# Copying the columns of the triangular inverse's outer products to PSUM in three parts

## The chip, the cores and the metric

The kernel runs on one core of one Trainium2 chip, as one program of five engines that work at the same time: TensorE (PE) for matrix products, VectorE (DVE), ScalarE (ACT) and GpSimd (POOL) for elementwise work, and SyncE (SP), which issues most DMAs. The metric is the device time of one execution in microseconds; the median of several executions is compared.

## What is computed

Three parts follow each other: an attention with a recurrent state, a layer of eight experts with one expert for each token, and a last layer of two products with a leaky ReLU. The change lies in the first part:

```python
def _attn_ref(r, k, v, w, a, b):
    for t in range(S):
        y[:, :, t] = einsum('bhd,bhde->bhe', rt, state)
        Sa = einsum('bhde,bhe->bhd', state, at)
        state = state * wt[:, :, None, :] - einsum('bhd,bhe->bhde', Sa, bt)
        state = state + einsum('bhd,bhe->bhde', vt, kt)
```

Here B = 4, H = 8, S = 768 and D = 40, all in float32. The expert layer has 3072 tokens of 320 values and 1024 hidden values for an expert, the last layer 2048 hidden values.

## The kernel before, in words

The recurrence is computed in chunks of `C` = 64 time steps. Inside a chunk the steps depend on each other through a lower triangular matrix, so each chunk needs the inverse of a unit triangular matrix of 64 x 64. Two batches and 256 time steps (four chunks) make one group; there are six groups, each with eight slots (four chunks, two halves of the heads), 48 slots in all. While the slots of one group run, the next group is prepared: `prepare` (decays by two scans on DVE, L455 and L457, and the scaled k, b and a, L460 and L464, on POOL), `products` (the matrices of a chunk, copied out of PSUM by ACT at L484 and L485 and masked by DVE at L491), and `inverse`. Each slot itself has stages that TensorE, ACT and DVE work on in turn: `stage_a` (L640, L642, L645), `stage_v` (L611, L613, L614), `stage_r` (L624, L628, L630), `stage_p` (L600, L602), `stage_c` (L656, L660, L661), `stage_d` (L676, L677), `stage_e` (L667, L671).

`inverse` treats a 64 x 64 triangle as two of 32 x 32. All triangles of 32 x 32 of a group are inverted at once: a transpose on DVE (L522) brings them into a tile `ul` of 128 partitions by 32 x 32, so that each partition holds one matrix. Then 31 steps follow, each an outer product (L529) of what is below the diagonal in column `j` of the matrix with the first `j + 1` values of row `j` of the unfinished inverse `ut`, into `tmp`, and a subtraction of `tmp` from the rows below (L531). Step `j` has `(31 - j) * (j + 1)` elements a partition, 31 to 256. Both are DVE instructions, and each depends on the one ahead of it. After the steps two checks on ACT (L424) and two transposes on DVE (L537, L538) follow, and then the halves are merged with products on TensorE (`zp` and `yp`, L557 and L565).

`ul` and `ut` lie in SBUF. `tmp` is a tile of 256 float32 values a partition in PSUM, in the one bank of tag `mg`, which the merges' `zp` and `yp` use too. Only the first group (`o.start`) differs: its `ut` lies in PSUM and its `tmp` in SBUF.

The program's order within each engine is not written by hand after the first group: a scheduler that goes through the program with estimates of its own sorts the instructions of each engine, and adds waits on semaphores where an instruction needs another engine's result or buffer. Each engine then works through its list strictly in order. `start_inverse` asks for the steps of group i + 1 at the first slot of group i. The dependencies are kept for each tile, a PSUM tile being one bank.

Of the kernel before, what the change touches and what calls it, by code (L numbers as in the profile page):

```python
# [8 lines left out]
F32 = mybir.dt.float32  # L9
# [10 lines left out]
P = 128  # L20
# [263 lines left out]
class Attention:  # L284
# [230 lines left out]
    def inverse(self, o):  # L515

        nc = self.nc
        l1, l2 = o.l1, o.l2
        o.tt = [self.ringed("tt", self.tt) for _ in range(2)]
        ut = self.ut0 if o.start else self.unit()  # L520
        ul = self.pa.tile([P, 32, 32], F32, name="ul", tag="t4", bufs=3)
        nc.vector.transpose(ul, l2.rearrange("p c u j -> p j (c u)"))  # L522
        yield
        for j in range(31):
            n, m = 31 - j, j + 1
            if j == 0 or o.start:
                tmp = self.pa.tile([P, 256], F32, name="tmp", bufs=1) if o.start else self.work("tmp", [P, 256], "mg")
            tv = tmp[:, :n * m].rearrange("p (a b) -> p a b", b=m)
            nc.vector.tensor_tensor(tv, ul[:, j, j + 1:].unsqueeze(2).to_broadcast([P, n, m]),  # L529
                                    ut[:, j, :m].unsqueeze(1).to_broadcast([P, n, m]), op=ALU.mult)  # L530
            nc.vector.tensor_tensor(ut[:, j + 1:, :m], ut[:, j + 1:, :m], tv, op=ALU.subtract)  # L531
            if j % 2:
                yield
        self.check(ut, ul, 0.01)
        self.check(l1.rearrange("p c u j -> p (c u) j"), ul, 0.01)
        t11, ttc = self.t4("t11"), self.t4("ttc")
        nc.vector.transpose(ttc.rearrange("p c u t -> p t (c u)"), ut)  # L537
        nc.vector.transpose(t11.rearrange("p c u s -> p s (c u)"), ut.rearrange("p t s -> p s t"))  # L538
        for half in range(2):
            for q in (1, 3, 0, 2):  # L540
                r = slice(32 * q, 32 * q + 32)
                eng = nc.vector if o.start and half == 0 else nc.gpsimd
                eng.tensor_scalar(o.tt[half][r, :, :, 32 * q:32 * q + 32], ttc[r, 2 * half:2 * half + 2], 1.0, 0.0, op0=ALU.mult, op1=ALU.add)
        yield

        lows = [slice(q * 64, q * 64 + 32) for q in range(2)]
        highs = [slice(q * 64 + 32, q * 64 + 64) for q in range(2)]
        both = [(c2, u, q) for c2 in range(2) for u in range(8) for q in range(2)]
        for half in range(2):
            if half:  # L550
                yield
            tt = o.tt[half]
            zp = self.work("zp", [P, 2, 8, 32], "w1" if o.start else "mg")
            if o.start:
                self.fill(zp, 8)
            for c2, u, q in both:
                nc.tensor.matmul(zp[lows[q], c2, u], lhsT=l1[highs[q], 2 * half + c2, u, :], rhs=tt[highs[q], c2, u, highs[q]], start=True, stop=True)  # L557
            z = self.pa.tile([P, 2, 8, 32], F32, name="z1", tag="z1", bufs=1)
            for lo in lows:
                nc.scalar.copy(z[lo], zp[lo])  # L560
            yp = self.work("yp", [P, 2, 8, 32], "w1" if o.start else "mg")
            if o.start:
                self.fill(yp, 8)
            for c2, u, q in both:
                nc.tensor.matmul(yp[lows[q], c2, u], lhsT=t11[lows[q], 2 * half + c2, u, :], rhs=z[lows[q], c2, u, :], start=True, stop=True)  # L565
            for lo, hi in zip(lows, highs):
                nc.scalar.activation(tt[lo, :, :, hi], yp[lo], AF.Copy, scale=-1.0)
            yield
# [755 lines left out]
```

## Time and profile before

| what | value |
| --- | --- |
| median of 3 runs | 1153.29 us (1152.75 to 1153.30) |
| the profiled execution, its own time | 1149.13 us |
| its span, first to last instruction | 1147.3 us |
| mean granted TensorE clock | 0.937 of full speed |
| PE busy | 1016.7 us, 89% of the span |
| DVE busy | 715.6 us, 62% |
| ACT busy | 568.4 us, 50% |
| POOL busy | 548.5 us, 48% |

The profile shows one execution. The attention takes about the first 515 us, the other two parts the rest. "Busy" is the time in which an engine has an instruction running, waits inside an instruction included. Shares over the whole span say little of one stretch, so the views below are cut to stretches. In the view of the chain, the work that ended last is followed back step by step to what released it, and each step is put down to an engine and a line; "issue" is time in which the engine waited for nothing that the profile shows.

### The profile page before, as it was taken

Reading aid. Unit: us, or ns where it says so; the run is one execution under the profiler, and the core shown is the slowest. Engines: PE = TensorE matmul, PEld = TensorE weight load, DVE = VectorE, ACT = ScalarE, POOL = GpSimd, SP = SyncE. Lnnn points to the kernel's source line nnn. Section 1 sums busy time; section 2 is a strip of 40 time slices with the busy share of each in tenths; the row PEclk is TensorE's granted clock in tenths of the full one; section 3 lists DMA queues with packets and bytes.
Section 4 is the critical chain, followed back from the end, with each engine's and each line's share of the span. In section 5 each row is a group of like instructions: output and inputs, shape, how many; then the busy total and the mean of one; then the engine's idle time right before and its main releaser. Section 6 shows DMA issues by size and latency. Waiting matters only on the chain.

```text
span 1147.3 us, 24800 instructions
## 1 busy us (share of the span) xinstructions
PE 1016.7 (89%) x9597; PEld 895.2 (78%) x9597; DVE 715.6 (62%) x1469; ACT 568.4 (50%) x1426; POOL 548.5 (48%) x496
## 2 busy tenths in 40 slices
PE   2649788989899889798898889999999999999997
PEld 2538677867687777687787779999998999999996
DVE  8865887878959869444599984324444545354542
ACT  3637577867787878783554444442222212121211
POOL 6717367555675724233655535452434343434332
PEclk7659899988999999799999989999999999999999
DMA  4613223322322213525688775431000000000000
GB/s 118 203 52 96 63 56 91 89 69 69 94 85 69 56 41 76 137 60 172 179 279 256 242 236 168 131 116 38 24 24 23 23 24 24 23 23 19 29 1 26
DMA packets 98080, 103.35 MB, mean 90 GB/s; under 512 B 58404, under 2 KB 78884, under 8 KB 97956
## 3 DMA queue, kind: packets, MB, share of 16 engines
q1 hardware_dynamic: 95652, 93.83, 28.5%
q0 software_dynamic: 2304, 7.87, 2.1%
q8 instruction: 78, 1.28, 0.5%
q14 instruction: 46, 0.38, 0.1%
HBM read 79.39 MB, written 22.28 MB: 89 GB/s over the span
## 4 chain that ended last, share of the span: by engine, by line
PE 57%; DVE 22%; ACT 6%; issue 5%; DMA 5%; POOL 3%; SPq 0%; DVEq 0%; ACTq 0%; POOLq 0%
PE ph L238 20%; PE po L238 19%; DVE tmp L529 3%; PE lp L483 3%; PE pp L600 2%; DVE ut L531 2%; PE sa L640 2%; PE yc L656 2%; DMA raw<-in_moe_w_dram 2%; DVE s L455 2%; DVE dec L215 2%; DVE dec L218 1%; PE rp L628 1%; DVE q L457 1%; DVE dec L214 1%
## 5 line engine op out<-in xcount | busy, mean ns | idle before, releaser
L229 POOL TENSOR_TENSOR gl<-g,gh 128x512 fp32r<-128x512 f32 x96 | 123.9, 1293 | 211.2 <-ACT gh L228 127.1
L228 ACT ACTIVATE gh<-g 128x512 fp32r<-128x512 f32 x96 | 60.7, 632 | 249.4 <-DVE g L1214 174.5
L1213 DVE TENSOR_SCALAR g<-ph,al 128x512 f32<-128x512 f32 x96 | 72.1, 751 | 156.9 <-POOL gl L229 79.1
L238 PE MATMUL ph<-x2thi,win 128*128 128x512 f32 x480 | 157.0, 392 | 0.0
L238 PE MATMUL po<-wout,gh 128*128 128x320 f32 x768 | 139.1, 309 | 0.0
L238 PEld LDWEIGHTS po<-wout,gh 128*128 128x128 f32 x768 | 122.0, 188 | 5.4
L238 PE MATMUL ph<-x2tlo,win 128*128 128x512 f32 x288 | 113.5, 394 | 0.0
L238 PE MATMUL po<-we,hh 128*128 128x320 f32 (+1 forms) x480 | 91.5, 319 | 19.1 <-DVE hh L1089 13.4
L238 PE MATMUL ph<-xthi,we 128*128 128x448 f32 (+2 forms) x360 | 98.2, 344 | 2.8 <-DVE hl L1089 2.1
L238 PEld LDWEIGHTS ph<-x2thi,win 128*128 128x128 f32 x480 | 88.5, 188 | 13.2
L238 PEld LDWEIGHTS po<-we,hh 128*128 128x128 f32 (+1 forms) x480 | 74.5, 183 | 24.7 <-DVE hh L1089 14.8
L529 DVE TENSOR_TENSOR tmp<-ul,ut 128x31 f32<-128x31 f32 (+15 forms) x186 | 81.4, 437 | 3.7
L238 PE MATMUL po<-wout,gl 128*128 128x320 f32 x384 | 82.9, 311 | 0.0
L614 POOL TENSOR_SCALAR_AFFINE_SELECT va<-vg 64x512 f32<-64x512 f32 x48 | 35.2, 734 | 85.2 <-ACT vg L613 55.8
L238 PE MATMUL ph<-xtlo,we 128*128 128x448 f32 (+2 forms) x216 | 74.1, 344 | 0.3 <-DVE xtlo L271 0.3
L238 PEld LDWEIGHTS ph<-xthi,we 128*128 128x128 f32 x360 | 67.0, 196 | 7.0 <-issue 2.5
L464 POOL TENSOR_TENSOR abd<-ra,q 40x512 f32<-40x512 f32 x44 | 62.4, 1418 | 18.9 <-DVE q L457 5.3
L483 PE MATMUL lp<-kb,abd 128*128 128x128 f32 x352 | 56.4, 307 | 16.7 <-DMA wz<-in_wP_dram 10.7
L1214 DVE SCALAR_TENSOR_TENSOR g<-ph,g 128x512 f32<-128x512 f32 x96 | 66.3, 691 | 3.1
L656 PE MATMUL yc<-va,kbr 128*40 128x104 f32 (+3 forms) x768 | 57.2, 265 | 11.8 <-issue 8.5
L600 PE MATMUL pp<-tt,la 128*104 128x128 f32 x384 | 61.4, 309 | 6.1 <-DVE lg L902 4.1
L677 POOL TENSOR_TENSOR yt<-rs,q 104x256 f32<-104x256 f32 x46 | 34.4, 748 | 67.6 <-DVE rs L676 54.5
(212 smaller groups left out, 2358.0 us busy)
## 6 DMA issues: line engine op xcount, KB each, us to landing
raw<-in_moe_w_dram SPq DMA_DIRECT2D x16, 512.0 KB
rv<-in_rvP_dram SPq DMA_DIRECT2D x48, 160.0 KB
raw<-in_moe_w_dram SPq DMA_DIRECT2D x16, 480.0 KB
kb<-in_kbP_dram SPq DMA_DIRECT2D x44, 160.0 KB
r<-in_moe_w_in_dram SPq DMA_DIRECT2D x10, 512.0 KB
r<-in_moe_w_out_dram SPq DMA_DIRECT2D x10, 512.0 KB
xs_d<-tt SPq DMA_DIRECT2D x8, 560.0 KB
raw<-in_moe_w_dram SPq DMA_DIRECT2D x16, 256.0 KB
```

What stands on the lines that cost most here:

```text
L228: nc.scalar.activation(hi, src, AF.Copy)
L229: return lo_eng.tensor_tensor(lo, src, f32(hi), op=ALU.subtract)
L238: return nc.tensor.matmul(out, lhsT=lhsT, rhs=rhs, start=start, stop=stop)
L464: nc.gpsimd.tensor_tensor(abd[r, :, q * C:(q + 1) * C], ra[r], qc[r, :, :C], op=ALU.mult)
L483: nc.tensor.matmul(lp[:, i], lhsT=abd[:, i, c2, :], rhs=kb[:, i, c2, :], start=True, stop=True)
L529: nc.vector.tensor_tensor(tv, ul[:, j, j + 1:].unsqueeze(2).to_broadcast([P, n, m]), ut[:, j, :m].unsqueeze(1).to_broadcast([P, n, m]), op ...
L600: nc.tensor.matmul(pp[:, i], lhsT=o.la[x.half][:, x.c2, u, :], rhs=o.tt[x.half][:, x.c2, u, :], start=True, stop=True)
L614: nc.gpsimd.affine_select(x.va[:C].rearrange("p a b c -> p (a b) c")[:, :, D:], x.vg[:C].rearrange("p a b c -> p (a b) c")[:, :, D:], patt ...
L656: nc.tensor.matmul(x.yc[r, i, a:], lhsT=kb[:, c], rhs=x.va[:, i, q, a:], start=True, stop=True)
L677: eng.tensor_tensor(yt[:PP, :, x.c2 * C:x.c2 * C + C], x.rs, x.o.q[x.half][:, x.p4, x.c2, :C], op=ALU.mult)
L1213: nc.vector.tensor_scalar(g, ph, 0.0, al[:, f:f + 1], op0=ALU.min, op1=ALU.mult)
L1214: nc.vector.scalar_tensor_tensor(g, ph, 0.0, g, op0=ALU.max, op1=ALU.add)
```

## The change

The steps of the five groups after the first read their column no longer from `ul` in SBUF, but from a copy in PSUM. The tile of tag `mg` grows from 256 to 512 values a partition, which is a whole bank: `tmp` is its first half, and the second half holds a part of `ul`. ACT copies that part three times in an inverse: ahead of step 0 the columns 0 to 7 (8 x 32 values), ahead of step 8 the columns 8 to 15 from row 8 on (8 x 24), ahead of step 16 the columns 16 to 31 from row 16 on (16 x 16). Each part is written over the one before. That is 15 new ACT instructions in the program. The first group's inverse is as before.

```diff
--- before.py
+++ after.py
@@ -523,10 +523,20 @@
         yield
         for j in range(31):
             n, m = 31 - j, j + 1
-            if j == 0 or o.start:
-                tmp = self.pa.tile([P, 256], F32, name="tmp", bufs=1) if o.start else self.work("tmp", [P, 256], "mg")
+            if o.start:
+                tmp = self.pa.tile([P, 256], F32, name="tmp", bufs=1)
+                col = ul[:, j, j + 1:]
+            else:
+                if j == 0:
+                    bank = self.work("tmp", [P, 512], "mg")
+                    tmp = bank[:, :256]
+                if j in (0, 8, 16):
+                    j0, j1 = j, (8, 16, 32)[j // 8]
+                    part = bank[:, 256:256 + (j1 - j0) * (32 - j0)].rearrange("p (a b) -> p a b", b=32 - j0)
+                    nc.scalar.copy(part, ul[:, j0:j1, j0:])
+                col = part[:, j - j0, j + 1 - j0:]
             tv = tmp[:, :n * m].rearrange("p (a b) -> p a b", b=m)
-            nc.vector.tensor_tensor(tv, ul[:, j, j + 1:].unsqueeze(2).to_broadcast([P, n, m]),
+            nc.vector.tensor_tensor(tv, col.unsqueeze(2).to_broadcast([P, n, m]),
                                     ut[:, j, :m].unsqueeze(1).to_broadcast([P, n, m]), op=ALU.mult)
             nc.vector.tensor_tensor(ut[:, j + 1:, :m], ut[:, j + 1:, :m], tv, op=ALU.subtract)
             if j % 2:
```

The new lines move what follows: the product, L529, is L539 in the changed file, the subtraction L531 is L541, and the copy is L536. The scheduler sorts the engines anew.

On DVE, at the start of the first pipelined inverse (the second group), this stood (`ul` is the matrix, `ut` the inverse, `tmp` the product; in brackets the engines whose progress an instruction waits for):

```order
L522 STREAM_TRANSPOSE ul<-l_670 128x1024 [waits Pool_49]
L529 TENSOR_TENSOR tmp<-ul,ut 128x31 [waits DVE_49]
L531 TENSOR_TENSOR ut<-ut,tmp 128x31 [waits DVE_49]
L529 TENSOR_TENSOR tmp<-ul,ut 128x60 [waits DVE_49]
L531 TENSOR_TENSOR ut<-ut,tmp 128x30x2 [waits DVE_49]
```

and now:

```order
L522 STREAM_TRANSPOSE ul<-l_670 128x1024 [waits Pool_49]
L539 TENSOR_TENSOR tmp<-tmp,ut 128x31 [waits Activation_49]
L541 TENSOR_TENSOR ut<-ut,tmp 128x31 [waits DVE_49]
L539 TENSOR_TENSOR tmp<-tmp,ut 128x60 [waits DVE_49]
L541 TENSOR_TENSOR ut<-ut,tmp 128x30x2 [waits DVE_49]
```

The first product now waits for ACT, right behind the transpose that ACT's copy needs, with nothing in between.

At steps 7 and 8 of the same inverse DVE had:

```order
L531 TENSOR_TENSOR ut<-ut,tmp 128x25x7 [waits DVE_49]
L457 SCALAR_TENSOR_TENSOR q<-wz_106,d1q_119 104x520 [waits DVE_49]
L529 TENSOR_TENSOR tmp<-ul,ut 128x192 [waits DVE_49]
L531 TENSOR_TENSOR ut<-ut,tmp 128x24x8 [waits DVE_49]
L529 TENSOR_TENSOR tmp<-ul,ut 128x207 [waits DVE_49]
L531 TENSOR_TENSOR ut<-ut,tmp 128x23x9 [waits DVE_49]
L529 TENSOR_TENSOR tmp<-ul,ut 128x220 [waits DVE_49]
```

and now:

```order
L541 TENSOR_TENSOR ut<-ut,tmp 128x26x6 [waits DVE_49]
L539 TENSOR_TENSOR tmp<-tmp,ut 128x175 [waits DVE_49]
L541 TENSOR_TENSOR ut<-ut,tmp 128x25x7 [waits DVE_49]
L539 TENSOR_TENSOR tmp<-tmp,ut 128x192 [waits DVE_49]
L541 TENSOR_TENSOR ut<-ut,tmp 128x24x8 [waits DVE_49]
L539 TENSOR_TENSOR tmp<-tmp,ut 128x207 [waits Activation_49]
L541 TENSOR_TENSOR ut<-ut,tmp 128x23x9 [waits DVE_49]
L539 TENSOR_TENSOR tmp<-tmp,ut 128x220 [waits DVE_49]
```

The product of step 8 (207 elements) now waits for ACT right behind the subtraction of step 7, and one scan and one mask stand earlier relative to the steps.

On ACT, near that second copy, this stood (`vg`, `rs`, `kbr`, `la` and `bds` belong to the slots and to the preparation of the group after):

```order
L630 COPY vg_406<-rp 40x4x64 [waits PE_49]
L630 COPY vg_406<-rp 40x4x64
L632 COPY rs<-rp 104x256
L504 COPY kbr<-bp 128x320 [waits PE_49]
L510 ACTIVATE la<-ap 64x4x40 [waits PE_49]
L510 ACTIVATE la<-ap 64x4x40
L671 COPY bds_411<-tp 40x2x40 [waits PE_49]
```

and now:

```order
L640 COPY vg_406<-rp 40x4x64 [waits PE_49]
L640 COPY vg_406<-rp 40x4x64
L642 COPY rs<-rp 104x256
L504 COPY kbr<-bp 128x320 [waits PE_49]
L536 COPY tmp<-ul 128x192 [waits DVE_49,Activation_49]
L510 ACTIVATE la<-ap 64x4x40 [waits PE_49]
L510 ACTIVATE la<-ap 64x4x40
L681 COPY bds_411<-tp 40x2x40 [waits PE_49]
```

The copy waits for DVE, and for ACT's own copy before; the two copies to `la` and those to `bds` are queued behind it.

## Rows read from the trace of the kernel before

**Rows 1.** Busy time by stretch, the five stretches of the pipelined inverses: engine, busy us (instructions)

```profile
core 0: us, PE busy (x) PEld busy (x) DVE busy (x) ACT busy (x) POOL busy (x), PEclk, DMA share, GB/s
...
sum 231.00, PE 202.38 PEld 168.52 DVE 214.82 ACT 161.02 POOL 109.86; mean PE 40.48 PEld 33.70 DVE 42.96 ACT 32.20 POOL 21.97
```

**Rows 2.** Chain of waits, shares by line, in the same five stretches, in their order

```profile
by line: DVE tmp L529 34.1%; DVE ut L531 22.0%; issue 10.6%; DVE q L457 6.0%; DVE va L645 5.8%; DVE ul L522 5.1%; ACT bds L671 2.3%; DVE la L491 1.7%; POOL l L490 1.6%; ACT va L642 1.5%; DVE yc L660 1.3%; DVE sm L661 1.2%; ACT kbr L504 1.1%
by line: DMA wz<-in_wP_dram 9.5%; issue 9.3%; PE pp L600 9.0%; DVE tmp L529 6.7%; PE yc L656 6.0%; DVE ut L531 5.3%; PE rvp L611 5.0%; DVE va L645 4.8%; DVE s L455 4.7%; PE rp L628 4.5%; PE sa L640 4.1%; PE xp L238 4.1%; PE lp L483 3.9%; DV
by line: PE yc L656 8.4%; issue 7.9%; PE xp L238 7.7%; DVE q L457 6.8%; PE pp L600 6.2%; PE lp L483 5.9%; PE sa L640 5.3%; PE rvp L611 5.2%; DVE tmp L529 4.6%; POOL xs_d L933 4.3%; PE ap L507 3.6%; DVE ut L531 3.5%; PE rp L628 3.2%; DVE s L
by line: DVE tmp L529 11.0%; PE pp L600 9.4%; DVE q L457 7.2%; issue 5.2%; PE rvp L611 4.8%; PE yc L656 4.5%; DVE s L455 4.5%; DVE ut L531 4.4%; DVE ttc L537 4.2%; POOL xs_d L933 4.2%; PE sa L640 3.6%; PE rp L628 3.3%; PE bp L503 2.9%; PE l
by line: DVE tmp L529 18.7%; DVE ut L531 13.4%; DVE va L645 10.7%; issue 5.9%; ACT va L642 5.8%; ACT bds L671 5.7%; PE sa L640 5.6%; DVE ttc L537 5.0%; PE xp L238 4.9%; ACT vg L624 3.6%; ACT tt L567 2.9%; DVE rs L676 2.5%; DVE yc L660 2.4%;
```

**Rows 3.** Busy time in these stretches of line 529 alone, then line 531 alone

```profile
sum 231.00, DVE 70.99; mean DVE 14.20
sum 231.00, DVE 51.52; mean DVE 10.30
```

**Rows 4.** One line's instructions, whole program: count, duration min/median/max in ns, first and last start

```profile
L529 DVE TENSOR_TENSOR tmp<-ul,ut x186: 188/394/2181, 39.0 to 450.9; 128x31 f32<-128x31 f32 x12, 128x60 f32<-128x60 f32 x12, 128x87 f32<-128x87 f32 x12, 128x112 f32<-128x112 f32 x12
L531 DVE TENSOR_TENSOR ut<-ut,tmp x186: 161/353/432, 39.2 to 451.2; 128x31 f32<-128x31 f32 x12, 128x60 f32<-128x60 f32 x12, 128x87 f32<-128x87 f32 x12, 128x112 f32<-128x112 f32 x12
```

**Rows 5.** Timeline of DVE, then POOL, near 379 us: start us, us, what

```profile
379.12 2.18 DVE L529 TENSOR_TENSOR tmp<-ul,ut 128x220 f32<-128x220 f32 x1
...
378.71 2.30 POOL L460 TENSOR_TENSOR kb<-kb,s 104x512 f32<-104x512 f32 x2
```

**Rows 6.** Timeline of DVE, then POOL, near 124 us

```profile
124.05 0.88 DVE L529 TENSOR_TENSOR tmp<-ul,ut 128x87 f32<-128x87 f32 x1
124.97 0.25 DVE L531 TENSOR_TENSOR ut<-ut,tmp 128x87 f32<-128x87 f32 x1
...
123.64 2.32 POOL L460 TENSOR_TENSOR kb<-kb,s 104x512 f32<-104x512 f32 x2
```

**Rows 7.** Groups by shape on DVE, 100 to 460 us: busy us, mean ns, idle us

```profile
L660 DVE TENSOR_TENSOR yc<-yc,sm 104x160 f32<-104x160 f32 x37 | 12.0, 326 | 5.6 <-PE yc L656 5.5
...
L529 DVE TENSOR_TENSOR tmp<-ul,ut 128x156 f32<-128x156 f32 x10 | 3.2, 324 | 0.2
...
L531 DVE TENSOR_TENSOR ut<-ut,tmp 128x156 f32<-128x156 f32 x10 | 3.1, 312 | 0.2
```

**Rows 8.** Groups by shape on ACT, 100 to 460 us, then 0 to 70 us

```profile
L613 ACT COPY vg<-rvp 64x256 f32<-64x256 f32 x78 | 28.6, 366 | 1.3
...
L319 ACT COPY ut<-zero 128x1024 f32<-128x1024 f32 x1 | 1.0, 1008 | 0.0
```

**Rows 9.** Timeline of all engines near 69 us

```profile
69.01 0.20 DVE L531 TENSOR_TENSOR ut<-ut,tmp 128x31 f32<-128x31 f32 x1
69.30 1.02 ACT L424 ACTIVATE ul<-ut 128x1024 f32<-128x1024 f32 x1 [3.99 <-DVE ut L531]
```

**Rows 10.** Who waited for whom on DVE, 100 to 460 us: us, times, longest us

```profile
DVE la L491 <- ACT l L485: 23.1, 10, 7.6
DVE q L457 <- ACT q L424: 10.7, 4, 5.1
DVE va L645 <- ACT va L642: 5.6, 11, 1.5
```

**Rows 11.** Groups by shape on DVE, 100 to 460 us: the lines that wait so

```profile
L491 DVE TENSOR_TENSOR la<-lp,negmask 128x256 f32<-128x256 f32 x37 | 15.5, 419 | 26.2 <-ACT l L485 23.1 <-PE pp L600 2.9
...
L645 DVE TENSOR_TENSOR va<-sa,posmask 64x256 f32<-64x256 f32 x76 | 32.1, 423 | 7.8 <-ACT va L642 5.6
...
L457 DVE TENSOR_TENSOR_SCAN q<-wz,d1q 104x520 f32<-104x520 f32 x16 | 25.5, 1594 | 11.1 <-ACT q L424 10.7
```

**Rows 12.** Chain of waits, shares by line, 452 to 560 us

```profile
by line: DMA raw<-in_moe_w_dram 18.7%; PE ph L238 8.2%; PE sa L640 6.0%; PE po L238 5.6%; POOL we L1040 5.6%; PE pp L600 5.0%; PE yc L656 4.4%; ACT we L1023 3.7%; PE rp L628 3.7%; issue 3.4%; ACT bds L671 3.3%; PE yp L565 3.1%; DMA raw<-xs_
```

## Prediction

> **What bounds the kernel now.** I read first the busy time of each engine by stretch, then the chain of waits inside the stretches that the change touches, then the two instructions of the inverse's step alone.
>
> The program runs six inverses, one for each group of 256 time steps; the change leaves the first (from 39 us on, under `o.start`) as it is and edits the other five. I cut five stretches round their steps: 120 to 158, 190 to 244, 266 to 317, 344 to 392 and 412 to 452 us, 231 us in all. VectorE (DVE) is busy for 214.8 of these 231 us, TensorE for 202.4, ScalarE (ACT) for 161.0 and GpSimd (POOL) for 109.9 [rows 1]. So DVE comes first, TensorE is close behind, and ACT has room. The chain of waits says where DVE sets the pace: in the first stretch the products (L529) hold 34.1% and the subtracts (L531) 22.0%, in the fifth 18.7% and 13.4%; in the second and third the chain goes mostly through TensorE's lines and the products hold 6.7% and 4.6%, in the fourth 11.0% [rows 2].
>
> Now the step itself. Product and subtract of a step have the same number of elements. Yet the 155 products of the five inverses take 70.99 us and their subtracts 51.52 us [rows 3]. The longest subtract took 432 ns, the longest product 2181 ns [rows 4]. What stretches a product is seen beside POOL: at 379.12 us one takes 2.18 us, from the start of a POOL pair on kb at 378.71 to its end at 381.01 [rows 5]; at 124.05 one of 87 elements takes 0.88 us inside such a pair that began at 123.64 [rows 6]. A product reads two tensors in SBUF, ul and ut; a subtract reads tmp in PSUM and ut in SBUF, and is never stretched: the one at 124.97 takes 0.25 us inside that same pair. So the products, and they alone of the step, wait for POOL's SBUF work. That costs 71.0 - 51.5 = 19.5 us of DVE.
>
> **The change part by part.**
>
> *Products read a PSUM column.* Each of the 155 now has one SBUF input, as the subtract has. I take the subtract's time: DVE gives back 19.5 us. The unstretched form could cost more with two PSUM sides. The nearest row is the addition at L660, PSUM and SBUF into PSUM, 160 elements: 326 ns; the product of 156 elements took 324 ns, the subtract 312 ns [rows 7]. From below the form costs nothing, from above the 14 ns between L660 and the subtract, 2.2 us for 155; I take nothing, since L660 has four elements more. [...]
>
> On the chain the share is smaller. By the percentages times the stretch, products less subtracts are 12.96 - 8.36 = 4.60 us in the first stretch, 3.62 - 2.86 = 0.76 in the second, 2.35 - 1.79 = 0.56 in the third, 5.28 - 2.11 = 3.17 in the fourth, 7.48 - 5.36 = 2.12 in the fifth: 11.2 us [rows 2]. The first and fifth, 6.7 us, I count whole. Of the other 4.5 I count three quarters, 3.4, since TensorE is next there: 202.4 of 231 us busy. Gain: **10.1 us**.
>
> *Fifteen copies on ACT.* Their own time: a copy of 256 elements a partition takes 366 ns (L613), one of 1024 from SBUF into PSUM 1008 ns [rows 8]; I take 0.37 us for each, 5.6 us in all. ACT has 70 us of idle time in these stretches, so this by itself costs nothing; if ACT had none, it would be those 5.6 us.
>
> *The new waits.* The second and third copy of an inverse overwrite the part before, and in the built program they wait for the subtract of step 7 and of step 15, not only for the product. So subtract, copy, product run one after the other. A hand-over takes about 0.1 us: the subtract at 69.01 ended at 69.21, ACT's check that waited for it began at 69.30 [rows 9]. One meeting costs 0.1 + 0.37 + 0.1 = 0.57 us of DVE where nothing stands between. In the new order that is so four times: all three meetings of the first pipelined inverse, and step 8 of the third. At two more, in the fifth, only two very short instructions stand between; I take 0.3 us for each. At the other nine DVE has work of other lines there. On the chain: 3 x 0.57 = 1.7 in the first, 0.1 for the third (its 4.6%), 0.3 in the fifth: **2.1 us**.
>
> *ACT may come late.* A copy stands in ACT's queue behind work that waits for TensorE or DVE. From below this is nothing, if ACT is always in time. For the rate I take DVE's existing waits for ACT, 23.1 + 10.7 + 5.6 = 39.4 us in 25 waits [rows 10], over the meetings there are: 37 for la, 16 for q, and 38 for va, whose 76 instructions come in pairs [rows 11]: 0.43 us a meeting. Fifteen make 6.5 us; the products' share of the chain is 31.7 of 71.0 us, 45%, so **2.9 us**. From above, each meets the mean of la's waits, 2.3 us.
>
> *ACT held by DVE.* A copy whose subtract isn't done holds ACT, and behind it the copies for la, bds, vg and pw that TensorE waits for. I price it at nothing, as ACT has idle time; it belongs to the bad case below.
>
> *Order.* The scheduler shifts other work round the copies: two scans on DVE come earlier in the first inverse, POOL's L543 later or earlier by some instructions, the loads on SP among each other. No row prices it; either way one POOL pair on kb, 2.3 us [rows 5], bounds what one such shift costs or brings. I take nothing.
>
> Sum: -10.1 + 2.1 + 2.9 = **-5.1 us**. The profiled execution took 1149.13 us, 4.2 us less than the median of 1153.29, so it would come to 1144.0 and the median to **1148.2**. What follows the attention starts from it: from 452 to 560 us the largest part of the chain is the experts' loads, 18.7% [rows 12], and these begin as the attention's buffers come free; I take the shift as passed on.
>
> About 0.2% (2.3 us) is what a measurement of this kernel can tell from no change.
>
> **The rivals.**
>
> - *Taken over by TensorE.* DVE gives back its time and TensorE, 88% busy, sets the stretches two to five as before. For it: the chain there goes through TensorE. Against: DVE is busy 93% over the five. Only the first stretch gains, 4.6 - 1.7 - 1.1 for lateness = 1.8 us: 1151.5.
> - *ACT's queue decides: slower.* At the fifteen meetings DVE waits 1.6 us (the mean of its 25 waits for ACT) to 2.3 us (the mean for la) more. On the chain 45% of 15 such waits is 10.8 to 15.5 us, with the 2.1 above, against 10.1: +2.8 to +7.6, 1156.1 to 1160.9. It decides from a mean of 1.2 us a meeting, where 0.45 x 15 x 1.2 = 8.1 eats the rest. For it: two queues in order, meeting where ACT has copies for TensorE ahead. Against: most of DVE's meetings with ACT pass without a wait.
> - *DVE alone bounds the stretches.* Then all of 19.5 counts, less 6.5 for lateness and 2.9 for the six uncovered meetings: -10.1, 1143.2. For it 93% busy; against it TensorE's share.
> - *Products still wait for POOL,* because two inputs in SBUF are not the reason. Then only the costs stay: +5.0, 1158.3. The subtracts, never above 432 ns, speak against it.
>
> **How the numbers follow.** The forecast gets 0.44 (its own range 1145.5 to 1151.5), TensorE taking over 0.20, ACT's queue 0.23, DVE alone 0.09, the products still waiting 0.04. Faster by over 0.2% is below 1151.0: 0.42 of the forecast, 0.09 and 0.03 of the second case, 0.54. Within 0.2%: 0.02 of the forecast and 0.17 of the second, 0.19. Slower: 0.23 + 0.04 = 0.27. The range runs from 1142 (DVE alone, a little better) to 1159 (into the case of ACT's queue) and leaves out the worst part of that and little else.
>
> **What would show it.** Right: the longest product near 0.45 us and the 155 at 52 us; DVE waits for the copies of 0.5 to 0.6 us in the first inverse; the first stretch shorter by 2 to 3 us. Wrong: products above 0.6 us beside POOL work; DVE waits for a copy of over 1.2 us on average; ACT idle at the copies while DVE is at something else; or the same stretches at unchanged length with more DVE idle time.

## The result and the profile after

| | before | changed |
| --- | --- | --- |
| median of 13 runs each | 1152.75 us (1146.12 to 1153.76) | 1141.03 us (1136.14 to 1150.03) |
| the profiled execution, its own time | 1149.13 us | 1138.26 us |
| its span | 1147.3 us | 1136.5 us |
| mean granted TensorE clock | 0.937 | 0.939 |

The ratio over all runs is 0.9913, with an interval of 0.989 to 0.9936: faster by 0.87%, 10.0 us [7.4 to 12.7]; the two medians alone give 0.9898. The forecast was a gain of 5.1 us, to 1148.2. From the 1153.29 us on which it stands, the ratio gives 1143.3 us [1140.6 to 1145.9]: inside the range of 1142 to 1159, near its lower end, and on the forecast side. The median of 1141.03 itself lies 1 us below the range. The gain is twice the sum.

The page of the changed kernel shows the engines and the chain over the whole span:

```profile
PE 1005.8 (88%) x9597; PEld 888.8 (78%) x9597; DVE 700.4 (62%) x1469; ACT 571.9 (50%) x1441; POOL 546.4 (48%) x496
...
PE 56%; DVE 19%; ACT 9%; issue 5%; DMA 5%; POOL 4%; SPq 1%; DVEq 0%; ACTq 0%; POOLq 0%
```

DVE is busy for 15.2 us less than the 715.6 us before, ACT 3.5 us more than 568.4.

The products, L539 (before L529) and L541 (before L531) answer to [rows 4]; the third line is the new copy. Columns: count, duration min/median/max in ns, first and last start.

```profile
L539 DVE TENSOR_TENSOR tmp<-tmp,ut x155: 188/367/433, 121.3 to 441.8; 128x31 f32<-128x31 f32 x10, 128x60 f32<-128x60 f32 x10, 128x87 f32<-128x87 f32 x10, 128x112 f32<-128x112 f32 x10
...
L541 DVE TENSOR_TENSOR ut<-ut,tmp x186: 160/355/432, 39.6 to 442.1; 128x31 f32<-128x31 f32 x12, 128x60 f32<-128x60 f32 x12, 128x87 f32<-128x87 f32 x12, 128x112 f32<-128x112 f32 x12
...
L536 ACT COPY tmp<-ul x15: 322/376/377, 120.9 to 425.3; 128x256 f32<-128x256 f32 x10, 128x192 f32<-128x192 f32 x5
```

The longest product was 2181 ns and is 433. The stretches of the five inverses are now 118 to 156, 183 to 237, 248 to 299, 336 to 381 and 402 to 443 us. Busy time in them, of all engines, then of L539 alone and of L541 alone, to be held against [rows 1, 3]:

```profile
sum 229.00, PE 209.06 PEld 176.26 DVE 203.57 ACT 176.13 POOL 110.30; mean PE 41.81 PEld 35.25 DVE 40.71 ACT 35.23 POOL 22.06
...
sum 229.00, DVE 53.44; mean DVE 10.69
...
sum 229.00, DVE 51.92; mean DVE 10.38
```

The products of the five inverses went from 70.99 to 53.44 us, 17.6 us less, and stand at 1.5 us over their subtracts. TensorE and DVE are now about equally busy there (209 and 204 of 229 us; before 202 and 215 of 231).

That POOL's work no longer reaches a product is seen where the two meet. The timeline of the first of these inverses, lines of L460 and L539 (start us, duration us, what):

```profile
121.86 3.25 POOL L460 TENSOR_TENSOR kb<-kb,s 104x512 f32<-104x512 f32 x2
...
122.26 0.26 DVE L539 TENSOR_TENSOR tmp<-tmp,ut 128x87 f32<-128x87 f32 x1
...
124.06 0.25 DVE L539 TENSOR_TENSOR tmp<-tmp,ut 128x112 f32<-128x112 f32 x1
...
124.66 0.31 DVE L539 TENSOR_TENSOR tmp<-tmp,ut 128x135 f32<-128x135 f32 x1
```

87 elements take 0.26 us beside the pair on kb; in [rows 6] the same shape took 0.88. Counted over the five inverses, 42 of the 155 products before are over 60 ns longer than the shortest of their shape, and a POOL instruction runs beside each of the 42. After, 80 products run beside POOL and none is that much longer.

What the change adds are waits. The waits of DVE from 110 to 450 us (us in total, times, longest), cut to those on ACT:

```profile
DVE la L491 <- ACT l L485: 22.7, 10, 9.0
DVE tmp L539 <- ACT tmp L536: 8.8, 11, 3.6
DVE va L655 <- ACT va L652: 5.4, 8, 1.7
DVE q L457 <- ACT q L424: 5.4, 3, 4.7
```

DVE waits 8.8 us for eleven of the fifteen copies. A meeting as the prediction described it, the second copy of the first inverse (timeline, in brackets the idle time before and what ended it):

```profile
129.78 0.35 DVE L541 TENSOR_TENSOR ut<-ut,tmp 128x192 f32<-128x192 f32 x1
...
130.22 0.32 ACT L536 COPY tmp<-ul 128x192 f32<-128x192 f32 x1 [0.89 <-DVE ut L541]
...
130.57 0.38 DVE L539 TENSOR_TENSOR tmp<-tmp,ut 128x207 f32<-128x207 f32 x1 [0.44 <-ACT tmp L536]
```

The subtract ends at 130.13, ACT begins 0.09 us later, ends at 130.54, and DVE begins 0.03 us later: 0.44 us. The longest wait, 3.59 us at the first copy of the third inverse, is a queue on ACT:

```profile
258.22 1.18 ACT L577 ACTIVATE tt<-yp 32x512 f32<-32x512 f32 x2
...
259.44 0.38 ACT L536 COPY tmp<-ul 128x256 f32<-128x256 f32 x1
...
259.90 0.20 DVE L539 TENSOR_TENSOR tmp<-tmp,ut 128x31 f32<-128x31 f32 x1 [3.59 <-ACT tmp L536]
```

The copy stands behind ACT's reading of yp, which lies in the bank mg that the copy writes: the merges of the inverse before must be out of the bank first.

**Where the time went.** From its first product to its last subtract an inverse took 34.8, 52.7, 49.2, 45.3 and 37.4 us before (122.41 to 157.21, 191.87 to 244.60, 267.63 to 316.83, 345.94 to 391.21, 414.00 to 451.38), and 33.9, 50.2, 38.5, 42.0 and 36.7 after (121.27 to 155.15, 186.46 to 236.64, 259.90 to 298.38, 338.94 to 380.97, 405.55 to 442.24): 18.1 us less in all. But the four gaps between them grew from 109.6 to 119.7 us, and of that the gap from the third to the fourth from 29.1 to 40.6. The lengths don't follow the products one by one: the products became 4.2, 3.0, 3.7, 4.8 and 1.7 us shorter, the inverses 0.9, 2.5, 10.7, 3.2 and 0.7. From the third the new order also moved work out: DVE's other lines take 29.4 us inside it before and 18.7 after. So lengths and gaps alone don't say what reached the end of the program. Marks outside the inverses do, the first mask (L645, now L655) of a slot; four slots before:

```profile
157.24 0.88 DVE L645 TENSOR_TENSOR va<-sa,posmask 64x256 f32<-64x256 f32 x2
...
250.93 0.88 DVE L645 TENSOR_TENSOR va<-sa,posmask 64x256 f32<-64x256 f32 x2
...
266.72 0.88 DVE L645 TENSOR_TENSOR va<-sa,posmask 64x256 f32<-64x256 f32 x2
...
516.11 0.88 DVE L645 TENSOR_TENSOR va<-sa,posmask 64x256 f32<-64x256 f32 x2 [1.17 <-ACT va L642]
```

and the same four after:

```profile
151.11 0.88 DVE L655 TENSOR_TENSOR va<-sa,posmask 64x256 f32<-64x256 f32 x2
...
234.92 0.42 DVE L655 TENSOR_TENSOR va<-sa,posmask 64x256 f32<-64x256 f32 x1
...
260.64 0.88 DVE L655 TENSOR_TENSOR va<-sa,posmask 64x256 f32<-64x256 f32 x2
...
507.16 0.88 DVE L655 TENSOR_TENSOR va<-sa,posmask 64x256 f32<-64x256 f32 x2 [1.18 <-ACT va L652]
```

These are slots 6, 15, 16 and the last (counted from 0; a slot has two masks): 6.1, 16.0, 6.1 and 8.9 us earlier. At slot 15 the changed kernel is far ahead, partly by order: the mark now stands ahead of the second inverse's last subtract (it ends at 236.64), and before it stood behind it (244.60). By slot 16 most of that lead is gone. From 235 to 262 us the chain goes through what prepares the third inverse:

```profile
by line: POOL tt L553 18.2%; DVE q L457 10.5%; DMA wz<-in_wP_dram 7.6%; PE sa L650 7.5%; DVE ttc L547 7.5%; DVE ul L522 6.8%; issue 6.4%; DVE s L455 6.0%; PE rvp L621 3.9%; PE pp L610 3.3%; DVE va L655 3.2%; POOL kb L460 3.1%; POOL yt L687 
```

The attention hands on 8.9 us of gain, and the span is 10.8 us shorter; the other 1.9 us come in the layers behind it and were not followed up.

### The profile page after: what moved, and what is told of

It reads as the page before. It is cut to its first block, busy times and chain, and to the rows that moved or that the text cites. A ratio compares the mean times of both kernels' runs of the same rounds, so it can differ in the third digit from the quotient of the medians.

```text
span 1136.5 us, 24811 instructions
## 1 busy us (share of the span) xinstructions
PE 1005.8 (88%) x9597; PEld 888.8 (78%) x9597; DVE 700.4 (62%) x1469; ACT 571.9 (50%) x1441; POOL 546.4 (48%) x496
## 4 chain that ended last, share of the span: by engine, by line
PE 56%; DVE 19%; ACT 9%; issue 5%; DMA 5%; POOL 4%; SPq 1%; DVEq 0%; ACTq 0%; POOLq 0%
PE ph L238 20%; PE po L238 19%; PE sa L650 2%; PE pp L610 2%; PE lp L483 2%; DMA raw<-in_moe_w_dram 2%; DVE ut L541 2%; DVE tmp L539 2%; PE yc L666 2%; DVE s L455 2%; DVE dec L215 2%; DVE q L457 2%; PE rp L638 1%; DVE dec L216 1%; POOL tt L553 1%
## 5 line engine op out<-in xcount | busy, mean ns | idle before, releaser
L238 PE MATMUL po<-we,hh 128*128 128x320 f32 (+1 forms) x480 | 91.8, 317 | 18.5 <-DVE hh L1099 13.7
L238 PEld LDWEIGHTS po<-wout,gl 128*128 128x128 f32 x384 | 64.1, 188 | 2.8
L541 DVE TENSOR_TENSOR ut<-ut,tmp 128x31 f32<-128x31 f32 (+15 forms) x186 | 62.7, 337 | 4.1
L483 PEld LDWEIGHTS lp<-kb,abd 128*128 128x128 f32 x352 | 47.9, 209 | 19.8 <-POOL abd L464 13.3
```

Source lines behind the costliest of these rows:

```text
L238: return nc.tensor.matmul(out, lhsT=lhsT, rhs=rhs, start=start, stop=stop)
L483: nc.tensor.matmul(lp[:, i], lhsT=abd[:, i, c2, :], rhs=kb[:, i, c2, :], start=True, stop=True)
```

## The experiments

Two theories. **Contention:** products with two inputs in SBUF are held by POOL's SBUF work, and reading the column from PSUM takes this away. **Order:** the copies make the scheduler sort the engines anew, and the new order brings the gain, wherever the products read. All ratios are against the kernel before on the same chip. That kernel's median was 1163.8, 1160.9, 1161.4 and 1150.9 us in the four sets of runs, so ratios are compared, not times. Percentages turned into us are of 1153. The edits are shown against the changed kernel where nothing else is said.

**The copies kept, the products back on ul.** This keeps the changed kernel's order on every engine, its copies and its waits.

```diff
-                col = part[:, j - j0, j + 1 - j0:]
+                col = ul[:, j, j + 1:]
```

> The fifteen copies to PSUM and all waits stay, and every engine's order is that of the changed kernel; only the products read their column from ul in SBUF again. Theory 1 (the gain is the products' waits for POOL's SBUF work): the 155 products take about 71 us again, the longest over 1 us, and the time is that of before or up to 6 us more, since the meetings with ACT stay: 1150 to 1159, ratio 0.998 to 1.006. Theory 2 (the gain is the new order of the engines): the order is the same, so the time stays within 3 us of the changed kernel, ratio 0.989 to 0.995.

Measured: 0.9988 [0.9962, 1.0014]. The products of the five inverses take 74.71 us, DVE waits 7.9 us for nine copies. Its products over the whole program:

```profile
L539 DVE TENSOR_TENSOR tmp<-ul,ut x186: 186/390/3058, 40.3 to 463.7; 128x31 f32<-128x31 f32 x12, 128x60 f32<-128x60 f32 x12, 128x87 f32<-128x87 f32 x12, 128x112 f32<-128x112 f32 x12
```

The long products are back, and the whole gain is gone. Against the changed kernel this run differs only in where a product reads; DVE, ACT, POOL and SP have the same instructions in the same order in both traces. The difference is 1 - 0.9913/0.9988 = 0.75%, 8.7 us [4.6 to 12.7]. The two ratios come from different chips; with the 0.9896 that the changed kernel shows in a later set, it is 0.92%. And the run prices all the costs at once, copies, waits and new order: -0.12% [-0.38, +0.14], or -1.4 us [-4.4 to +1.6], where the prediction had +5.0. The 74.71 us of its products are 3.7 more than the 70.99 before the change, and this too is part of the -1.4.

**The copies on DVE.** No meeting with ACT is left on the way from subtract to product.

```diff
-                    nc.scalar.copy(part, ul[:, j0:j1, j0:])
+                    nc.vector.tensor_copy(part, ul[:, j0:j1, j0:])
```

> The three copies of an inverse are made by DVE instead of ACT, so no product waits for ACT; DVE gets 15 copies of some 0.33 us, 5 us. Theory 1: products unstretched at 52 us, the 8.8 us of waits for ACT gone, 5 us of work in their place, so 0 to 4 us faster than the changed kernel: ratio to before 0.987 to 0.992. Theory 2: the order is another one again, so the time can lie anywhere from 0.99 to 1.003. Theory 3 (the meetings with ACT cost most of what the products gain): over 5 us faster than the changed kernel, ratio below 0.987.

Measured: 0.993 [0.9899, 0.9961]; products 53.48 us. Its copies, and what DVE waited for ahead of them:

```profile
L536 DVE COPY tmp<-ul x15: 350/410/428, 124.2 to 435.4; 128x256 f32<-128x256 f32 x10, 128x192 f32<-128x192 f32 x5
...
  ACT tt L577: 8.1, 2
```

The fifteen copies take 6.0 us (421 ns each with 256 elements, 358 with 192), where some 0.33 us each and 5 us in all were expected. Two first copies now wait 8.1 us together on DVE for ACT to empty the bank mg: the long wait of the changed kernel belongs to the bank and not to ACT's copying. The time is the changed kernel's within the intervals.

**Copies that nobody reads.** The kernel before, with ACT copying the same columns into an SBUF tile of its own.

```diff
+            if not o.start and j in (0, 8, 16):
+                j1 = (8, 16, 32)[j // 8]
+                idle = self.pa.tile([P, 256], F32, name="idle", bufs=1)
+                nc.scalar.copy(idle[:, :(j1 - j) * (32 - j)].rearrange("p (a b) -> p a b", b=32 - j), ul[:, j:j1, j:])
```

> The kernel before, with the fifteen ACT copies going to an SBUF tile that nothing reads: ACT's work and a shifted order of the engines, with products as before. Theory 1: no gain, 1150 to 1156, ratio 0.998 to 1.003, products at 71 us. Theory 2: an order that shifts moves the time by several us by itself, ratio outside 0.997 to 1.003.

Measured: 0.9998 [0.9969, 1.0028]; products 72.3 us. ACT's time for the copies, together with the new order that they bring, costs nothing that can be measured.

**One copy for an inverse.** One DVE copy of eight columns, with no meeting after the first step. It leaves out the second and third part: from step 8 on a product reads a column of the first part, so the attention's numbers differ.

```diff
-                if j in (0, 8, 16):
-                    j0, j1 = j, (8, 16, 32)[j // 8]
-                    part = bank[:, 256:256 + (j1 - j0) * (32 - j0)].rearrange("p (a b) -> p a b", b=32 - j0)
-                    nc.scalar.copy(part, ul[:, j0:j1, j0:])
-                col = part[:, j - j0, j + 1 - j0:]
+                if j == 0:
+                    part = bank[:, 256:].rearrange("p (a b) -> p a b", b=32)
+                    nc.vector.tensor_copy(part, ul[:, :8])
+                col = part[:, j % 8, j + 1:]
```

> One copy of eight columns by DVE in each inverse, ahead of step 0, and every product reads its column from it (steps 8 and on take a wrong column, so the numbers of the attention differ): products with one SBUF input and no meeting with ACT. Theory 1: products at 52 us, 1.7 us of DVE copies, no waits: 1 to 5 us faster than the changed kernel, ratio 0.986 to 0.991. Theory 2: the order differs from both kernels, ratio anywhere from 0.99 to 1.003. Theory 3: over 5 us faster than the changed kernel, ratio below 0.986.

Measured: 0.9966 [0.9943, 0.999]; products 53.35 us. Products as fast as the changed kernel's and ten copies fewer, and yet less gain: 0.53% less than the 0.9913. Either the meetings bring something, which no mechanism explains, or its order is a worse one. A twin for this run and one for the DVE copies, with their order kept, tell these apart.

**The changed kernel again,** in the set of these twins, unedited:

> The changed kernel unaltered, on the chip of this set, beside its twins. All theories: ratio 0.989 to 0.994, as before; the products at 52 to 54 us.

Measured: 0.9896 [0.9854, 0.9938], waits for the copies 8.5 us in eleven. The result holds on another chip.

**Twin of the DVE copies,** with its order on every engine, the products on ul:

```diff
-                    nc.scalar.copy(part, ul[:, j0:j1, j0:])
-                col = part[:, j - j0, j + 1 - j0:]
+                    nc.vector.tensor_copy(part, ul[:, j0:j1, j0:])
+                col = ul[:, j, j + 1:]
```

> The kernel with DVE's copies, in the same order on every engine, but the products read their column from ul in SBUF (the copies stay and nothing reads them). Theory 1: the products go back to 70 us and over and the time loses all that e2 gained and DVE's 5 us of copies: ratio 0.999 to 1.006. Theory 2 (order): as e2, 0.990 to 0.996.

Measured: 1.0074 [1.0048, 1.0101], a little above the expected range. Its products:

```profile
L539 DVE TENSOR_TENSOR tmp<-ul,ut x186: 186/384/3786, 38.7 to 473.9; 128x31 f32<-128x31 f32 x12, 128x60 f32<-128x60 f32 x12, 128x87 f32<-128x87 f32 x12, 128x112 f32<-128x112 f32 x12
```

76.14 us of products in the five inverses against 53.48, and 1.43% [1.0, 1.8] of time, 16.5 us, between the twins. The granted TensorE clock differs too, 0.923 in the mean of this run's executions against 0.930 with the products on the copy; part of the 16.5 us may come by way of TensorE, and no run splits it.

**Twin of the one copy,** again with the order kept (against the run with one copy):

```diff
-                col = part[:, j % 8, j + 1:]
+                col = ul[:, j % 8, j + 1:]
```

> The kernel with one copy in each inverse, in the same order on every engine, but the products read the column from ul in SBUF (of steps 8 and on the same wrong columns as in e5). Theory 1, with an order that itself loses about 5 us: products at 70 us and over, ratio 1.002 to 1.007, that is 0.006 to 0.010 above e5. Theory 2 (order alone): as e5, 0.994 to 0.999. Theory 4 (in e5's order the products' waits are off the path): as e5 too, with products at 70 us.

Measured: 1.0059 [1.0033, 1.0086]; products 75.16 us. Between the twins 0.92% [0.6, 1.3], 10.7 us. So that order, with one small DVE copy an inverse and products 4.2 us longer than before the change, is 0.59% slower than before: the products' source is worth no less in it, and the order is why the run with one copy gained less.

**Only the first copy of an inverse on DVE,** to take the meeting at the bank away from ACT:

```diff
-                    nc.scalar.copy(part, ul[:, j0:j1, j0:])
+                    (nc.scalar.copy if j else nc.vector.tensor_copy)(part, ul[:, j0:j1, j0:])
```

> The changed kernel with the first copy of each inverse on DVE and the other two on ACT: the waits for the first copy (4.5 us of the 8.8 us) become 5 copies of some 0.33 us. Theory 1: 0 to 4 us faster than the changed kernel, unless the new order loses it; ratio 0.985 to 0.993. Theory 2: anywhere from 0.985 to 1.003.

Measured: 0.9936 [0.9907, 0.9965]. DVE waits 3.8 us for six ACT copies, and 6.2 us in two waits for ACT to empty the bank. No gain over the changed kernel.

**Twice the meetings.** Each part is copied a second time by ACT, between its steps, at two choices of steps. The first:

```diff
+                if j in (4, 12, 24):
+                    nc.scalar.copy(part, ul[:, j0:j1, j0:])
```

> The changed kernel with six copies in each inverse: each part is copied a second time, over itself, ahead of steps 4, 12 and 24, so DVE and ACT meet 30 times instead of 15. If a meeting costs what the prediction took (5.0 us for 15 on the chain), 15 more cost 5 us: ratio 0.994 to 0.998. If meetings cost little in this kernel: 0.988 to 0.993. An order that moves the time by itself by 5 us can blur either.

The second, with `j in (3, 11, 20)`:

> The same with the second copies ahead of steps 3, 11 and 20: another order of the engines with the same count of meetings. Ratio 0.994 to 0.998 if meetings cost what the prediction took, 0.988 to 0.993 if they cost little; the distance to the run before it shows what order alone does.

Measured: 0.9956 [0.9928, 0.9985] and 1.0042 [1.0009, 1.0074]; the second lies outside both of its expected ranges. DVE's waits for the copies in the first run (L536 is the old copy, L538 the added one):

```profile
DVE tmp L541 <- ACT tmp L536: 17.0, 11, 7.7
DVE tmp L541 <- ACT tmp L538: 4.5, 8, 1.4
```

and in the second:

```profile
DVE tmp L541 <- ACT tmp L538: 4.5, 7, 1.1
DVE tmp L541 <- ACT tmp L536: 4.2, 6, 1.8
```

The run that waits 21.5 us is 0.86% faster than the one that waits 8.7 us. The pair was to price a meeting and can't: the two differ in the order that the scheduler made, and that is worth more than the waits. Their products take 53.5 and 53.6 us, so POOL is not the reason; the slower one ran at a mean granted TensorE clock of 0.922 against 0.929, which may be a part of it.

**The second and third copy on DVE, the first on ACT:**

```diff
-                    nc.scalar.copy(part, ul[:, j0:j1, j0:])
+                    (nc.vector.tensor_copy if j else nc.scalar.copy)(part, ul[:, j0:j1, j0:])
```

> The changed kernel with the first copy of each inverse on ACT and the other two on DVE: five meetings with ACT and ten DVE copies (3 us). If the products' waits for POOL are what counts: within 4 us of the changed kernel, ratio 0.987 to 0.995; if the meetings for the second and third copy were dear (4.3 us of waits): below 0.987.

Measured: 0.9888 [0.9843, 0.9933]; waits for the copies 4.8 us, in four. Half the waits of the changed kernel, and a time that can't be told from it.

**Other cuts.** The parts end at columns 9, 20 and 32, and lie at the end of the bank.

```diff
-                if j in (0, 8, 16):
-                    j0, j1 = j, (8, 16, 32)[j // 8]
-                    part = bank[:, 256:256 + (j1 - j0) * (32 - j0)].rearrange("p (a b) -> p a b", b=32 - j0)
+                if j in (0, 9, 20):
+                    j0, j1 = j, {0: 9, 9: 20, 20: 32}[j]
+                    part = bank[:, 512 - (j1 - j0) * (32 - j0):].rearrange("p (a b) -> p a b", b=32 - j0)
```

> The changed kernel with its three parts cut at steps 9 and 20 instead of 8 and 16 (9 x 32, 11 x 23 and 12 x 12 values): the same count of copies and meetings, the same kind of products, another order of the engines. If the order of the changed kernel is nothing special: ratio 0.988 to 0.993. If it happens to be a good one, which pays for its meetings: 0.994 to 0.998, that is 4 to 5 us nearer to the kernel before.

Measured: 0.991 [0.9878, 0.9941], waits 10.2 us in twelve. With other cuts and another order the gain is the same within the intervals, so it doesn't hang on these places. No version beats the changed kernel by more than the intervals.

## Why the prediction was right in sign and short in size

*Products wait for POOL's SBUF work: right.* Three pairs with the same order in each and only the product's source changed differ by 8.7, 16.5 and 10.7 us. The reading of [rows 5] was loose: that product ends at 381.30 us, 0.29 us behind the end of the POOL pair, and not with it. The products fell to 53.44 us where 52 was forecast, the longest to 433 ns where 0.45 us was. The rival that products still wait fell with this.

*The form with PSUM on two sides at no cost: nearly.* Product and subtract differ by 53.44 - 51.92 = 1.5 us over 155, 10 ns each, inside the bounds of 0 to 14 ns. The shortest product takes 188 ns with either source.

*Gain on the chain, 10.1 us: right as a size.* In the change's own order it measures 8.7 us [4.6 to 12.7]. But the pair takes away 21.3 us of DVE time (74.71 - 53.44), not 19.5, and in the other two some 22 us (76.14 - 53.48, 75.16 - 53.35) are worth 16.5 us in one order and 10.7 in another, so the closeness to 10.1 is partly luck.

*Copies free on ACT: right.* 376 and 322 ns each, and the copies that nobody reads, with their order, cost nothing measurable.

*The new waits, 2.1 us, and ACT coming late, 2.9 us: the step that failed.* As waits of DVE they were sized well: 6.5 of lateness and 2.9 for the six uncovered meetings made 9.4 us, and 8.8 were measured. The mean is 0.6 us a copy, half of the 1.2 at which the rival of ACT's queue decides; that rival fell. What failed is adding 5.0 us for these waits to the time, with the new order at nothing beside them. The run with the products back on ul carries such waits, 7.9 us, and ends within -4.4 to +1.6 us of the kernel before, and not 5.0 later. The weight of 45% was the products' share of the chain before. After the change the steps hold far less of it: the chain's shares by line in the five stretches (now cut to the first and the last) read

```profile
by line: DVE ut L541 11.8%; DVE tmp L539 9.8%; issue 6.5%; POOL abd L464 6.2%; PE sa L650 5.6%; PE pp L610 5.4%; DVE va L655 4.5%; ACT vg L623 3.4%; ACT vg L634 3.3%; ACT tt L577 3.1%; ACT va L652 3.0%; ACT ul L424 2.8%; PE rp L638 2.7%; PE
...
by line: PE sa L650 13.2%; PE pp L610 10.3%; PE yc L666 9.9%; PE rvp L621 6.0%; PE rp L638 5.9%; PE warm L238 4.9%; PE xp L238 4.8%; ACT vg L634 4.7%; ACT bds L681 3.9%; issue 3.9%; DVE ut L541 3.8%; PE tp L677 3.2%; ACT vg L623 3.1%; ACT p
```

against 34.1% and 18.7% for the products in [rows 2]. Over the five the products hold 15.6 of 53.4 us, 29%, and of the fifteen copies five stand on the chain, with 1.9 us. That a wait in a place that the chain has left costs little is argued from this; no run shows it by itself.

And it can't be the whole of it. The run with the products on ul has nine copies on its chain, 3.2 us, its products hold 40.5 of 74.7 us there, more than the 45% before, and it is not slower than before. Something in the new order must pay for its meetings; what that is stays open.

*Order, priced at nothing with a bound of 2.3 us: the bound was too small.* Order with little else moved the time by +0.59% (the twin of the one copy) and by 0.86% (the two runs with twice the meetings), 7 to 10 us; with the copies that nobody reads it moved nothing measurable. The forecast's missing 5 us are, as far as the runs show, the sum of cheap waits and what the new order brings; they don't split the two, since every edit that takes a meeting away makes the scheduler sort anew.

*The rival of DVE alone: its number came true, its working didn't.* It forecast 1143.2 us, and the ratio gives 1143.3. But it counted all 19.5 us of the products as gain and all 9.4 us of waits as loss, where the pair with the order kept shows 8.7 us for the products' 21.3 and no net cost of the rest. That it hits the time is a coincidence.

*The stretches.* Of the gain on the chain 6.7 us were placed in the first and the fifth stretch; the inverses there became 0.9 and 0.7 us shorter, and the third, in part by order, 10.7. The first was to become 2 to 3 us shorter. From first product to last subtract it is 0.9 us shorter; the slot of the mark at 157.24 us comes 6.1 earlier, but its place in the order moved too, so the mark says little for this stretch alone. The waits there are 0.67, 0.44 and 0.50 us, against 0.5 to 0.6 expected. That TensorE takes over is right for the fifth stretch and was too dark for the total: 1151.5 was forecast in that case.

Left open: why the changed kernel is 16.0 us ahead at slot 15 and 6.1 at slot 16, and why its fourth inverse begins only 7.0 us earlier than before when its third ends 18.5 earlier. The chain between these two inverses, from 298.4 to 338.9 us, is spread over many lines, none above 6% but for issue with 10%, and no run was made for it.

## What to carry to other kernels

Where a VectorE operation with both inputs in SBUF runs beside GpSimd's SBUF work, look at its longest time against a like operation with one PSUM input: here the surplus, 17.6 of 71.0 us, went away with one input copied to PSUM on an engine that had room. Show such an effect with a twin that keeps the order of every engine and changes only where the operand is read, since a scheduler's new order alone can move a kernel by as much as the effect. A wait that a change adds is better not added to the sum at the weight that the old chain gives its place: here that made 5.0 us, and the net of all costs measured -1.4.

## What the runs showed of the hardware that was not expected

- At the second copy of the first inverse the hand-over from ACT's copy to DVE took 0.03 us, the one from DVE to ACT 0.09 us, so this full meeting cost 0.44 us with a copy of 0.32.
- With the column in SBUF single products took up to 2.18 us before, that one beside POOL's pair on kb, and up to 3.06 and 3.79 us in two twins, where no view here shows what ran beside these two. With the column in PSUM they took 0.43 us at most, though 80 of the 155 ran beside POOL.
- Over the fifteen copies from SBUF to PSUM the median was 376 ns on ACT and 410 ns on DVE.
- The longest wait for a copy, 3.59 us, came from the shared bank: the copy stood behind ACT's reading of yp, and moving it to DVE moved the wait with it (8.1 us in two waits).
